# Softmax sum by identity matmuls, bf16 exponentials, other masks, two q,k loads and a new operation order in a one-core attention and mixer block

## The chip, the cores and the metric

The kernel runs on one core of a Trainium2 chip. The metric is the device time of one execution in microseconds (us); the median of a few executions is given. One further execution is recorded by the hardware profiler, and all rows of the profile come from that one. The core has five engines with a queue each: PE (matmuls; its weight loads appear as PEld), DVE (VectorE), ACT (ScalarE), POOL (GpSimd) and SP, which here issues the DMAs. Each engine works through its queue in order and waits on semaphores.

## The reference

Sequence length is 2048, width 448, all inputs and the output bf16. It is a pre-layernorm block with attention over a dilated window and then a mixer with an MLP:

```python
def _A_ref(x, wqkv, wo):                       # x is layernorm(A_x)
    H = 16; Dh = D // H                        # Dh = 28
    W, dil = 8, 2
    q, k, v = qkv[0], qkv[1], qkv[2]           # from x @ wqkv
    idx = pos[:, None] - (jnp.arange(W) * dil)[None, :]
    mask = idx >= 0
    logits = jnp.einsum("bhsd,bhswd->bhsw", q, kg) * scale      # kg = k at idx
    logits = jnp.where(mask[None, None, :, :], logits, -1e9)
    attn = _softmax(logits, axis=-1)           # over the 8 window entries
    o = jnp.einsum("bhsw,bhswd->bhsd", attn, vg)
    return o.reshape(B, S, D) @ wo
...
def _B_ref(x, w1, w2, w3, w4):                 # x is layernorm(h)
    h = _gelu(_layernorm(x) @ w1)
    hs = concat(four column groups of h, moved by 1, -1, 2, -2 rows) @ w2
    x1 = x + hs
    return x1 + _gelu(_layernorm(x1) @ w3) @ w4
...
h = x + _A_ref(_layernorm(x), A_wqkv, A_wo)
return h + _B_ref(_layernorm(h), B_w1, B_w2, B_w3, B_w4)
```

Only tokens 0 to 13 have window entries before the start of the sequence; for them the first-token mask matters.

## The kernel before

The 2048 rows are four tiles of 512. For each tile t these phases run: N1 (layernorm of x), A1 (q and k, transposed), V, A2 (logits), S (softmax), A3 (attention times v), O (wo and residual), B1 (second norm, w1 and gelu, called M). Then five units of 2, 4, 4, 4 and 2 row tiles of 128 go through B2 (the four shifted column groups times w2, and a norm called T), W3 (w3 and gelu into `h3T`) and B3 (w4 and the store).

**Recording and order.** Every phase first records operations (`S.add`, `S.group`); an operation is one instruction, or a group of matmuls. The list `ORDER` at the top of the file then gives one global sequence of operation numbers. `arrange` walks it, hands out buffers (8 PSUM banks, 3 `qk_r` buffers, 1 softmax buffer) and appends each operation to the queue of its engine, so `ORDER` decides what stands before what on PE, DVE, ACT, POOL and SP. `OTHER` lists operations that go to their alternative engine (an ACT copy to DVE, a DVE operation to POOL). All instructions are emitted at one line, L1014 (L1013 in the changed kernel), so the profile is read by names of tiles and by shapes.

**Pairs of half-height matmuls.** `duo` (L463) forms two outputs A and B whose contraction rows are split into upper and lower 64 partitions. Matmuls of the two halves alternate, so that they run as pairs, and a duo has two parts: in the second part the outputs change halves, and it waits by semaphore (`sdeps`) for the end of the first part. For V a duo is 8 matmuls and then 6; for q, k it is 8 and 6 per 512 columns. `ORDER` may put something else between the two parts, or nothing: then a row such as "x28" in the order of PE is two duos back to back.

**Softmax of a tile (L744 to L793).** A2 multiplies q by the eight shifted k on DVE (`qk_r`, 128x4096, in four chunks of channels, the last 128x2048), and PE sums over channels with the 0/1 matrix `zc` into one PSUM bank L (matmuls 128 rows by 32 columns of the array). For tile 0 the bank is started by a one-row matmul of `onesrow` and `maskrow` with 512 columns, which adds -30000 at the entries before the sequence. S takes the maximum on DVE (`mx<-ps`), subtracts (`ls<-ps,mx`), takes exp on ACT (`ls<-ls`, f32), sums over the window on DVE (`mx<-ls`), forms 1/sum as exp(-ln(sum)) on ACT (`mx<-mx`, twice), and multiplies on DVE (`pb<-ls,mx`). PE transposes `pb` with `ident` (80 columns), and the result is copied to `pt`.

**Attention times v.** A3 multiplies `pt` by a 0/1 band mask `bmask` on DVE (`bd_r`, 80x2048, four per tile) and PE multiplies `vw` by it in 32 matmuls (80 rows by 32 columns of the array). `bmask` is made at the start in `setup` (L609): POOL fills a table `par` (memset and one affine_select of 80x80), and two DVE reduces turn it into `bmask`.

**Loads.** SP issues, in this order, x in three DMAs (rows 0 to 511), q,k weights in four DMAs of 128x2x448 (two halves of the rows, q and k apart), x for tile 1 in two, v weights in two, and so on (from L436). In B2, units from the third on read shifted halves `ht`, which SP copies from `gT` (named `arena` in the trace) by seven DMAs.

## Time and profile before

| | value |
|---|---|
| median of 3 executions | 189.06 us (188.81 to 189.17) |
| the profiled execution's own time | 188.75 us |
| its span on the core | 187.0 us |
| PE busy | 179.8 us (96%) |
| DVE busy | 127.2 us (68%) |
| ACT busy | 121.8 us (65%) |
| POOL busy | 24.0 us (13%) |

The profiled execution took 188.75 us, of which 187.0 us are the span in which the core's instructions run and 1.75 us lie around it; it is 0.31 us below the median. PE is the busiest engine by far. DVE and ACT are full in the first 77 us, in which attention runs, and half empty after it. A row of the timeline gives the start, the length, the engine, the line, the operation with out<-in, the array tile (rows*columns) and the moving operand, a count, and in brackets the idle time before it with its releaser. Matmul records overlap: a duration in a row of one matmul includes the time in the array, so the pace of a run of matmuls is read from the starts of neighbouring rows.

### The profile page before, as it was taken

To read this page: it belongs to the slowest core of one execution; us is meant where nothing else is said; L and a number is where in the kernel's file an instruction comes from. 1 tells how busy PE (TensorE), PEld (TensorE's weight loads), DVE (VectorE), ACT (ScalarE), POOL (GpSimd) and SP (SyncE) were. 2 spreads that over 40 slices of the span, in tenths; PEclk is the share of its full clock that TensorE was granted. 3 is DMA by queue.
4 is the path that set the end of the run, shared out by engine and by line. 5 is a ranking of instruction groups with operands and counts; after the bars stand their busy time and mean duration, and the time that the engine had idled before them with its cause. 6 is when DMAs were issued, how large, how long until landed. Compare 5 with 4: busy or idle time off the path is not lost.

```text
span 187.0 us, 5780 instructions
## 1 busy us (share of the span) xinstructions
PE 179.8 (96%) x2496; PEld 93.4 (50%) x2496; DVE 127.2 (68%) x225; ACT 121.8 (65%) x289; POOL 24.0 (13%) x59
## 2 busy tenths in 40 slices
...
GB/s 153 314 297 189 14 91 124 186 192 34 154 75 112 112 227 160 298 52 101 16 112 7 38 25 22 94 133 53 35 40 40 116 0 46 112 0 4 49 98 49
DMA packets 34177, 18.59 MB, mean 99 GB/s; under 512 B 21240, under 2 KB 33640, under 8 KB 34152
## 3 DMA queue, kind: packets, MB, share of 16 engines
...
q8 instruction: 19, 0.31, 0.7%
q14 instruction: 6, 0.05, 0.1%
...
## 4 chain that ended last, share of the span: by engine, by line
PE 76%; DVE 14%; DMA 3%; SPq 3%; ACT 2%; issue 1%
PE ps L1014 76%; DVE qk_r L1014 9%; SPq L1014 3%; DMA xin<-in_A_x_dram 2%; DVE st L1014 2%; DVE lntm L1014 1%; ACT arena L1014 1%; DMA ht<-arena 1%; DVE mx L1014 1%; DVE ls L1014 0%; DVE pb L1014 0%; DVE mv L1014 0%; ACT actT L1014 0%; ACT rs_x L1014 0%; ACT rs_y L1014 0%
## 5 line engine op out<-in xcount | busy, mean ns | idle before, releaser
L1014 PE MATMUL ps<-actT,arena 64*128 64x512 bf16 (+2 forms) x812 | 69.6, 326 | 0.9 <-DMA arena<-in_A_wqkv_dram 0.5
L1014 ACT ACTIVATE h3T<-ps 128x512 bf16<-128x512 f32 (+1 forms) x70 | 30.9, 517 | 37.3 <-PE ps L1014 37.2
L1014 PEld LDWEIGHTS ps<-actT,arena 64*128 64x128 bf16 (+1 forms) x812 | 36.0, 96 | 30.9 <-PE ps L1014 1.9
L1014 PE MATMUL ps<-arena,h3T 64*128 64x448 bf16 (+3 forms) x434 | 44.7, 343 | 0.1
L1014 ACT ACTIVATE arena<-ps 128x512 bf16<-128x512 f32 (+6 forms) x66 | 30.6, 508 | 8.7 <-PE ps L1014 8.1
L1014 PEld LDWEIGHTS ps<-arena,h3T 64*128 64x128 bf16 (+1 forms) x434 | 22.3, 94 | 19.9 <-PE ps L1014 0.5
L1014 DVE TENSOR_TENSOR qk_r<-arena 128x4096 bf16<-128x4096 bf16 (+1 forms) x16 | 32.0, 2015 | 0.0
L1014 DVE SCALAR_TENSOR_TENSOR qk_r<-ps,mrs,arena 128x448 bf16<-128x448 f32 (+2 forms) x17 | 10.4, 653 | 30.8 <-PE ps L1014 30.8
L1014 POOL TENSOR_TENSOR arena<-arena,xin 128x448 f32<-128x448 f32 x16 | 16.1, 1033 | 78.6 <-ACT lntm L1014 66.0
L1014 DVE TENSOR_TENSOR bd_r<-arena,bmask 80x2048 bf16<-80x2048 bf16 x16 | 19.0, 1216 | 2.6 <-PE ps L1014 2.6
L1014 DVE SCALAR_TENSOR_TENSOR arena<-xin,rs_y,ps 128x448 f32<-128x448 bf16 x16 | 10.3, 673 | 11.6 <-PE ps L1014 11.5
L1014 PE MATMUL ps<-wo_s,actT 64*128 64x448 bf16 x128 | 14.5, 350 | 0.1
L1014 PE MATMUL ps<-actT,w_s 64*112 64x512 bf16 x112 | 13.8, 380 | 0.1
L1014 PE MATMUL ps<-w_s,arena 64*128 64x448 bf16 x83 | 12.8, 350 | 0.4 <-DMA ht<-arena 0.3
L1014 ACT ACTIVATE actT<-ps 128x512 bf16<-128x512 f32 (+2 forms) x20 | 12.3, 640 | 1.0 <-PE ps L1014 0.9
L1014 PE MATMUL ps<-arena,actT 64*128 64x448 bf16 x112 | 12.3, 351 | 0.2
L1014 ACT ACTIVATE lntm<-xin,nm 128x448 bf16<-128x448 bf16 x16 | 10.6, 666 | 1.4 <-DVE nm L1014 1.4
L1014 DVE BATCH_NORM_STATS2 st<-xin 128x6 f32<-128x448 bf16 x16 | 9.2, 613 | 1.3 <-DMA xin<-in_A_x_dram 1.3
L1014 ACT ACTIVATE rs_x<-mv,epsilon 128x4 f32<-128x4 f32 (+2 forms) x16 | 4.6, 297 | 7.4 <-DVE mv L1014 7.3
L1014 PEld LDWEIGHTS ps<-actT,w_s 64*112 64x112 bf16 x112 | 6.8, 127 | 5.2 <-ACT arena L1014 0.7
L1014 ACT ACTIVATE vt<-ps 128x448 bf16<-128x448 f32 x16 | 8.2, 544 | 1.2 <-PE ps L1014 1.1
L1014 PEld LDWEIGHTS ps<-w_s,arena 64*128 64x128 bf16 x83 | 5.5, 95 | 6.8 <-DMA ht<-arena 0.8
...
## 6 DMA issues: line engine op xcount, KB each, us to landing
...
```

Of the source, the lines that this page charges most:

```text
L1014: inst = getattr(eng, meth)(**kw)
```

## The change

The sum over the eight window entries leaves DVE: exp is written as bf16 (`es_b`), and eight matmuls with the full 128x128 `ident` as weights, 64 columns each, add the eight entries in PSUM. They write the first 64 columns of bank L, the bank that held the logits. ACT's logarithm reads the sum there, 1/sum is written as bf16 (`zr_b`), and the product `pb` reads two bf16 operands.

`bmask` is written by POOL alone: a memset and eight affine_selects of 80x64; the two DVE reduces are gone. The first-token mask becomes a matmul of 128 rows, 32 columns of the array and 98 moving columns inside the first logit group of tile 0 (`onesrow` and `maskrow` get 128 partitions, and only the first has ones and -30000). The q and k weights are loaded by two DMAs of 128x2x896.

`ORDER` is written anew for all engines; operation numbers differ by the recorded operations that were added and dropped. `OTHER` has three entries more (four are added and one is dropped): a second copy `actT<-ps` of tile 0's transposed norm and two small copies of 128x48 (`arena<-arena`) go from ACT to DVE, the multiplication `pb` of the last tile goes from DVE to POOL, and one copy of the last tile's `pt` stays on ACT.

```diff
--- before.py
+++ after.py
@@ -18,40 +18,40 @@
 RESIDUAL = 'ttvv'
 DENSE = 2
 ORDER = """
-2 5 6 0 1 41 42 43 8 9 7 10 52 53 54 57 12 13 14 4 55 56 58 15 16 35 44 31 64 62 38 39 17 45 65 63 36 46 59 60
...
+0 5 6 8 1 9 44 45 2 7 55 56 57 60 46 47 48 10 65 38 41 67 29 61 49 58 66 62 63 68 69 70 50 51 52 53 54 59 92 64
...
 """
 OTHER = """
-94 184 187 485 494 497 548 554
+97 99 186 189 238 350 484 493 496 550 556
 """
 FULL = (4,)
 FILL = (0, 0, 0, 0)
@@ -343,6 +343,8 @@
         epsilon = sb("epsilon", [128, 2], F32)
         mx = sb("mx", [128, NSM, 64], F32)
         ls = sb("ls", [128, NSM, 512], F32)
+        es_b = sb("es_b", [128, NSM, 512], BF16)
+        zr_b = sb("zr_b", [128, NSM, 64], BF16)
         zs = mx
         indj = ls[:, NSM - 1, 0:40].bitcast(BF16).rearrange("p (c h) -> p c h", c=5)
         pb = sb("pb", [128, NSM, NW * KW], BF16)
@@ -369,8 +371,8 @@
         kk = [arv(A_KV + t * KVB, 128, 3 * KVW).rearrange("p (c n) -> p c n", c=3) for t in range(NST)]
         kr = [arv(A_KV + t * KVB + 3 * KVW, 128, 4 * KW).rearrange("p (j n) -> p j n", j=4) for t in range(NST)]
         pt = [arv(A_KV + t * KVB + 4 * KVW, KW, 1024) for t in range(NST)]
-        maskrow = arv(A_KV + (NST - 1) * KVB, 1, 512)
-        onesrow = arv(A_KV + (NST - 1) * KVB + 512, 1, 32)
+        maskrow = arv(A_KV + (NST - 1) * KVB, 128, 512)
+        onesrow = arv(A_KV + (NST - 1) * KVB + 512, 128, 32)
         xb = [arv(A_KV + i // 4 * KVB, 128, 4 * D * 2).bitcast(F32).rearrange("p (i d) -> p i d", d=D)[:, i % 4, :] for i in range(NTL)]
 
         def shifted(t, c):
@@ -438,10 +440,7 @@
             load_x(i, 1)
         load_x(2, 2)
         act(zs[:, 0, 0:1], epsilon[:, 0:1], ACT.Exp)
-        for h in range(2):
-            for g in range(2):
-                dma("w%s%s" % ("qk"[g], "ab"[h]), wqkv_s[:, 2 * h:2 * h + 2, g * D:(g + 1) * D],
-                    A_wqkv[192 * h:192 * h + 256, g * D:(g + 1) * D].rearrange("(c k) n -> k c n", k=128), 256 * D * 2)
+        load_rows("wqk", wqkv_s[:, :, 0:2 * D], A_wqkv, 0, 2 * D)
         load_x(4, 2)
         load_x(6, 2)
         load_rows("wv", wqkv_s[:, :, 2 * D:3 * D], A_wqkv, 2 * D, D)
@@ -608,12 +607,10 @@
 
         def setup():
 
-            par = ls[0:KW, 0, 128:168].bitcast(BF16).rearrange("p (e j) -> p e j", e=2)
-            pool("memset", ap=par, constant=0.0)
-            pool("affine_select", out=par, in_=par, pattern=[[1, 2], [2, KW // 2]], compare_op=ALU.not_equal, fill=1.0, base=0, channel_multiplier=-1)
-            for e in range(2):
-                dve("tensor_reduce", out=bmask[:].rearrange("p (m e r) -> p m e r", m=4, e=2)[:, :, e, :],
-                    in_=bass.AP(par.tensor, par.offset + e * (KW // 2) + 1, [list(par.ap[0]), [8, 4], [1, NW], [1, 8]]), axis=AX.X, op=ALU.max)
+            pool("memset", ap=bmask[:], constant=0.0)
+            for w in range(NW):
+                pool("affine_select", out=bmask[:], in_=bmask[:], pattern=[[16, 4], [1, 2], [DIL, NW]], compare_op=ALU.not_equal, fill=1.0,
+                     base=DIL * (w + 1), channel_multiplier=-1)
             pool("memset", ap=indj, constant=1.0)
             for out_ap, pat, base in ((indj[:, 0:4, :], [[128, 4], [-DH, 16]], 0), (indj[:, 4, :], [[-DH, 16]], 320)):
                 pool("affine_select", out=out_ap, in_=out_ap, pattern=pat, compare_op=ALU.is_ge, fill=0.0, base=base, channel_multiplier=1)
@@ -635,7 +632,7 @@
             late("memset", ap=maskrow, constant=0.0)
             for w in range(1, NW):
                 lo = DIL * (NW - 1 - w)
-                late("memset", ap=maskrow[:, 0:64 * w].rearrange("p (r n) -> p r n", n=64)[:, :, lo:lo + DIL], constant=-30000.0)
+                late("memset", ap=maskrow[0:1, 0:64 * w].rearrange("p (r n) -> p r n", n=64)[:, :, lo:lo + DIL], constant=-30000.0)
             late("memset", ap=kk[0][:, :, 0:PADK], constant=0.0)
             late("memset", ap=kr[0][0:64, 0, 0:PADK], constant=0.0)
             late("memset", ap=vw[0:PADK, 0, 0, :], constant=0.0)
@@ -747,8 +744,6 @@
             sl = t % NSM
             held = []
             L = _Tile(P_bank)
-            if t == 0:
-                mm(L(lambda v: v[0:32, :]), onesrow[0:1, :], maskrow[0:1, :], True, False, 512)
             for c in range(4):
                 wide = 8 if c < 3 else 4
                 r = _Tile(P_qk)
@@ -762,7 +757,10 @@
                                       zc[:, c, e, :],
                                       r(lambda v, lo=lo: bass.AP(v.tensor, v.offset + lo + 64 * (NW - 1),
                                                                  [list(v.ap[0]), [16, 4], [-64, NW], [DIL, NW], [1, DIL]])),
-                                      c == 0 and e == 0 and not (t == 0 and j == 0), c == 3, 512, j))
+                                      c == 0 and e == 0, c == 3, 512, j))
+                if t == 0 and c == 0:
+                    first = lambda v: v.rearrange("p (r n) -> p r n", n=64)[:, 0:NW - 1, 0:DIL * (NW - 1)]
+                    terms.append((L(lambda v: first(v[0:32, :])), onesrow, first(maskrow), False, False, 98, 0))
                 op = mms(terms)
                 if t == NST - 1:
                     product_read.append(op)
@@ -773,13 +771,14 @@
             all_x = lambda v: y_e(v).unsqueeze(2).broadcast_to([128, 32, NW, DIL])
             dve("tensor_reduce", out=y_e(mx[:, sl, :]), in_=L(e_x), axis=AX.X, op=ALU.max)
             dve("tensor_tensor", out=x_e(ls[:, sl, :]), in0=L(x_e), in1=all_x(mx[:, sl, :]), op=ALU.subtract)
-            act(ls[:, sl, :], ls[:, sl, :], ACT.Exp, scale=SCALE)
-            dve("tensor_reduce", out=y_e(zs[:, sl, :]), in_=e_x(ls[:, sl, :]), axis=AX.X, op=ALU.add)
-            act(zs[:, sl, :], zs[:, sl, :], ACT.Ln)
-            act(zs[:, sl, :], zs[:, sl, :], ACT.Exp, scale=-1.0)
+            act(es_b[:, sl, :], ls[:, sl, :], ACT.Exp, scale=SCALE)
+            mms([(L(lambda v: v[:, 0:64]), ident[:], es_b[:, sl, :].rearrange("p (y x e) -> p x y e", x=NW, e=DIL)[:, x], x == 0, x == NW - 1, 64, None)
+                 for x in range(NW)])
+            act(zs[:, sl, :], L(lambda v: v[:, 0:64]), ACT.Ln)
+            act(zr_b[:, sl, :], zs[:, sl, :], ACT.Exp, scale=-1.0)
             row = lambda v, off, step: bass.AP(v, off, [[v.shape[1] * v.shape[2], 128], [step, NW], [16, 4], [DIL, NW], [1, DIL]])
-            mult = dict(out=row(pb, sl * NW * KW + DIL, KW + DIL), in0=row(ls, sl * 512, 64),
-                        in1=bass.AP(zs, sl * 64, [[64 * NSM, 128], [8, NW], [2, 4], [0, NW], [1, DIL]]), op=ALU.mult)
+            mult = dict(out=row(pb, sl * NW * KW + DIL, KW + DIL), in0=row(es_b, sl * 512, 64),
+                        in1=bass.AP(zr_b, sl * 64, [[64 * NSM, 128], [8, NW], [2, 4], [0, NW], [1, DIL]]), op=ALU.mult)
             S.add("dve", "tensor_tensor", alts=[("pool", [("tensor_tensor", mult)])], **mult)
             banks = [_Tile(P_bank), _Tile(P_bank)]
 
```

What the new order does is seen in the queues. In the rows, a shape is what the instruction writes, and x28 is a count of equal rows.

On PE at the start, from the first q,k matmuls of tile 0 (`ps<-actT,arena`) over V (`ps<-arena,actT`) to the first logit sums (`ps<-qk_r,zc`); before:

```order
L1014 MATMUL ps<-actT,arena 128x256 x72
L1014 MATMUL ps<-actT,arena 64x256 x28
L1014 MATMUL ps<-actT,arena 128x256 x6
L1014 MATMUL ps<-ident,lntm 128x64 x16
L1014 MATMUL ps<-actT,arena 128x256 x6
L1014 MATMUL ps<-ident,lntm 128x64 x16
L1014 MATMUL ps<-arena,actT 128x448 x28
L1014 MATMUL ps<-actT,arena 128x512 x28
L1014 MATMUL ps<-arena 32x512
L1014 MATMUL ps<-qk_r,zc 32x32x8x2 x8
```

and in the changed kernel:

```order
L1013 MATMUL ps<-actT,arena 128x256 x64
L1013 MATMUL ps<-arena,actT 128x448 x8
L1013 MATMUL ps<-actT,arena 128x256 x8
L1013 MATMUL ps<-arena,actT 128x448 x6
L1013 MATMUL ps<-ident,lntm 128x64 x32
L1013 MATMUL ps<-actT,arena 128x256 x12
L1013 MATMUL ps<-arena,actT 128x448 x14
L1013 MATMUL ps<-actT,arena 64x256 x16
L1013 MATMUL ps<-actT,arena 128x512 x8
L1013 MATMUL ps<-actT,arena 64x256 x40
L1013 MATMUL ps<-actT,arena 128x512 x8
L1013 MATMUL ps<-qk_r,zc 32x32x8x2 x8
```

V of tile 0, 28 matmuls in one piece before, now stands in pieces of 8, 6 and 14 among the q,k matmuls, and the q,k duos of tile 1 are split too. The mask matmul, ahead of the logit sums before, follows the last row shown.

On DVE, around the softmax of tile 0 and the products of tile 1; before:

```order
L1014 TENSOR_REDUCE mx<-ps 128x64
L1014 TENSOR_SCALAR nm<-mv 128x4
L1014 TENSOR_TENSOR ls<-ps,mx 128x512
L1014 TENSOR_TENSOR qk_r<-arena 128x4096
L1014 TENSOR_REDUCE mx<-ls 128x64
L1014 TENSOR_TENSOR qk_r<-arena 128x4096
L1014 TENSOR_TENSOR qk_r<-arena 128x2048
L1014 TENSOR_TENSOR pb<-ls,mx 128x8x64
L1014 TENSOR_TENSOR qk_r<-arena 128x4096
L1014 TENSOR_TENSOR bd_r<-arena,bmask 80x2048
```

and in the changed kernel:

```order
L1013 TENSOR_REDUCE mx<-ps 128x64
L1013 TENSOR_TENSOR qk_r<-arena 128x4096
L1013 TENSOR_SCALAR nm<-mv 128x4
L1013 TENSOR_TENSOR ls<-ps,mx 128x512
L1013 TENSOR_TENSOR qk_r<-arena 128x4096
L1013 TENSOR_TENSOR qk_r<-arena 128x2048
L1013 TENSOR_TENSOR pb<-es_b,zr_b 128x8x64
L1013 TENSOR_TENSOR qk_r<-arena 128x4096
L1013 TENSOR_TENSOR bd_r<-arena,bmask 80x2048
```

The reduce `mx<-ls` is gone, and the first product of tile 1 has moved ahead of the subtraction. On PE the eight sums of this tile (`ps<-es_b,ident`) stand between the first logit sums of tile 1 and the 28 q,k matmuls of tile 2.

On PE, where the third unit's shifted halves `ht` are first used; before:

```order
L1014 MATMUL ps<-actT,arena 128x512 x14
L1014 MATMUL ps<-bd_r,vw 32x64 x64
L1014 MATMUL ps<-wo_s,actT 128x448 x8
L1014 MATMUL ps<-actT,arena 128x512 x6
L1014 MATMUL ps<-wo_s,actT 128x448 x24
L1014 MATMUL ps<-w_s,arena 128x448
L1014 MATMUL ps<-w_l,ht 128x448
```

and in the changed kernel:

```order
L1013 MATMUL ps<-actT,arena 128x512 x8
L1013 MATMUL ps<-bd_r,vw 32x64 x64
L1013 MATMUL ps<-wo_s,actT 128x448 x8
L1013 MATMUL ps<-actT,arena 128x512 x6
L1013 MATMUL ps<-wo_s,actT 128x448 x24
L1013 MATMUL ps<-arena,h3T 128x448 x14
L1013 MATMUL ps<-w_s,arena 128x448
L1013 MATMUL ps<-w_l,ht 128x448
```

Fourteen matmuls of B3 (`ps<-arena,h3T`) now stand between the last wo matmuls of tile 3 and the first use of `ht`.

60 rows, old and new, of the table ORDER are left out of this document.

## The prediction

> **What bounds the kernel now.** I read the busy time by stretch first. The columns are the stretch, its length, and the busy time (with instruction counts) of PE, PEld, DVE, ACT and POOL, then the granted clock, the DMA share and GB/s.
>
> ```profile
> 8.30:35.00 26.70, 25.98 (x367) 13.18 (x367) 25.78 (x39) 23.12 (x63) 1.68 (x17) 1.00 0.66 152
> 35.00:62.00 27.00, 26.75 (x548) 12.68 (x552) 26.97 (x40) 24.78 (x67) 0.00 (x0) 1.00 0.55 118
> 62.00:77.00 15.00, 14.85 (x272) 7.98 (x265) 14.86 (x18) 14.68 (x34) 0.99 (x1) 1.00 0.76 193
> 77.00:110.00 33.00, 32.51 (x514) 18.16 (x514) 24.23 (x51) 24.73 (x53) 6.42 (x10) 1.00 0.31 75
> 110.00:184.60 74.60, 74.50 (x780) 39.15 (x776) 28.77 (x63) 30.29 (x66) 12.13 (x14) 1.00 0.25 54
> ```
>
> From 8.3 us to 184.6 us PE is idle for only 0.72 + 0.25 + 0.15 + 0.49 + 0.10 = **1.71 us**. So the time is PE's own work plus these 1.71 us, plus 8.3 us ahead of that and the 2.4 us up to the span's end at 187.0. The granted clock is 1.00 in every stretch. DVE is as full as PE between 8.3 and 77 us, so it can hold PE up there, but nowhere else. Next, pieces of the chain that ended last (start, length, what), and a row of PE's waits (total, times, longest):
>
> ```profile
> 28.25 0.59 DVE mx L1014
> ...
> 32.78 2.21 DVE qk_r L1014
> 34.99 0.04 issue
> 35.04 2.84 PE ps L1014 x58
> PE ps L1014 <- DMA ht<-arena: 0.3, 1, 0.3
> ```
>
> These chain rows stand where DVE hands over: up to 34.99 us DVE carries the chain, then PE. DVE time saved before 35 us can therefore move the end, and DVE time saved after that hardly at all.
>
> **The change part by part.** I count PE's own work first, then its idle time.
>
> *The pace of PE.*
>
> ```profile
> 13.85 0.40 PE L1014 MATMUL ps<-ident,lntm 64*128 64x64 bf16 x16
> 14.08 0.49 PE L1014 MATMUL ps<-actT,arena 64*128 64x256 bf16 x6
> ...
> 14.64 3.29 PE L1014 MATMUL ps<-arena,actT 64*128 64x448 bf16 x28
> 17.77 3.19 PE L1014 MATMUL ps<-actT,arena 64*128 64x512 bf16 x28
> 20.89 0.38 PE L1014 MATMUL ps<-arena 1*32 1x512 bf16 x1
> 21.20 0.62 PE L1014 MATMUL ps<-qk_r,zc 128*32 128x512 bf16 x8
> ...
> 38.68 0.42 PE L1014 MATMUL ps<-bd_r,vw 80*32 80x64 bf16 x32
> 39.03 0.93 PE L1014 MATMUL ps<-arena,actT 64*128 64x448 bf16 x8
> 71.22 0.43 PE L1014 MATMUL ps<-bd_r,vw 80*32 80x64 bf16 x32
> 71.47 0.63 PE L1014 MATMUL ps<-qk_r,zc 128*32 128x512 bf16 x8
> 115.01 6.78 PE L1014 MATMUL ps<-arena,h3T 64*128 64x448 bf16 x70
> 121.64 1.89 PE L1014 MATMUL ps<-actT,w_s 64*112 64x512 bf16 x16
> ```
>
> A pair of 448 columns costs (121.64 - 115.01)/35 = 0.189 us. Fourteen pairs of V should then take 2.65 us, but tile 0's V takes 17.77 - 14.64 = 3.13 us: 0.48 us more for two duos whose second part follows its first directly, 0.24 us each. That is what a duo pays when nothing stands between its parts, since the second part waits for the end of the first. A change of array shape costs about 0.10 us: 32 band matmuls take 0.35 us among half-height ones (38.68 to 39.03) and 0.25 us next to the logit sums (71.22 to 71.47), which have the same 32 columns.
>
> *Adjacent duo parts.* In the order of PE 12 duos have their parts directly behind one another before, and 6 do in the changed kernel. Six fewer at 0.235 us: **-1.41 us**. Below I take the new pieces between the parts to be long enough (8 to 28 matmuls) to cover the wait.
>
> *Identity sums.* 4 x 8 = 32 matmuls of 128x128 weights and 64 columns are added. No such shape is in the trace. From below: pairs of half-height matmuls of 64 columns pace at (14.08 - 13.85)/8 = 29 ns. From above, this row of PEld, whose columns are busy us, mean ns of one, and idle time:
>
> ```profile
> L1014 PEld LDWEIGHTS ps<-ident,lntm 128*128 128x128 bf16 x16 | 0.9, 98 | 1.8 <-DVE lntm L1014 1.7
> ```
>
> Sixteen full-height loads keep PEld busy 0.9 us, 56 ns each, under matmuls of 128 columns; one alone lasts 98 ns. So 29 to 56 ns if loads overlap as there, up to 98 ns if not: +0.93, +1.8 or +3.1 us. I take 29 ns, **+0.93 us**, since 128 columns explain the 56 ns of that row as well as its loads do.
>
> [...]
>
> *Array shapes.* PE changes shape 47 times before and 52 times after, since the sums stand among half-height matmuls: 5 x 0.10 = **+0.5 us**.
>
> *Mask matmul.* 512 columns took 21.20 - 20.89 = 0.31 us, of which 0.21 is its columns; 98 columns at the same rate are 0.04: **-0.17 us**. The next logit sums no longer stand behind it.
>
> PE's own work: -1.41 + 0.93 + 0.5 - 0.17 = **-0.15 us**.
>
> *The start.* PE waited 0.48 us at 8.32 for the last q,k weights:
>
> ```profile
> 8.32 5.69 PE L1014 MATMUL ps<-actT,arena 64*128 64x256 bf16 x106 [0.48 <-DMA arena<-in_A_wqkv_dram]
> 2.20 2.00 SPq L1014 DMA_DIRECT2D arena<-in_A_wqkv_dram  x4
> 6.86 1.62 ACT L1014 ACTIVATE actT<-ps 128x512 bf16<-128x512 bf16 x3 [0.20 <-PE ps L1014]
> ```
>
> Two issues of about 0.5 us each leave SP, so everything behind is issued some 1.0 us earlier, but the same bytes move. If the weights come earlier, the copies of the transposed tile 0 are next: ACT's end at 8.48. One of its three copies, 0.54 us each, goes to DVE, which brings this down. From -0.5 to +0.4 (a larger DMA that lands later as a whole); I take **-0.2 us**.
>
> *DVE up to 35 us.* The reduce at 28.25 goes, 0.59 us. More of the chain, and of PE's timeline:
>
> ```profile
> 13.98 0.32 issue
> 35.04 0.83 PE L1014 MATMUL ps<-qk_r,zc 128*32 128x512 bf16 x12 [0.21 <-DVE qk_r L1014]
> ```
>
> The chain's pause of 0.32 us at 13.98 is filled as well, since the new order puts four BN_STATS ahead of the first product where two stood. DVE gains 0.59 + 0.32 = 0.9 us by 35 us. PE can use only what it waits for there: 0.21 us for a product at 35.04, and its idle 0.72 us between 8.3 and 35 us. I take **-0.5 us**, between nothing and -0.7. DVE's work saved after 35 us I cost at nothing: its rivals there are PE's queue and the 0.25 + 0.15 us that PE idles.
>
> *The ht wait.* PE waited 0.32 us for `ht` at 109.28. Fourteen matmuls of B3, 7 x 0.189 = 1.3 us, now stand in front: **-0.3 us**, next late is nothing that the trace shows. A store now stands between SP's ht issues; at 0.5 us like the issues below, the 1.3 us cover it.
>
> *New waits.* PE now waits for exp at four points, and everything in its queue waits behind.
>
> ```profile
> L1014 DVE TENSOR_REDUCE mx<-ps 128x64 f32<-128x512 f32 x4 | 2.7, 680 | 0.0
> L1014 DVE TENSOR_TENSOR ls<-ps,mx 128x512 f32<-128x512 f32 x4 | 2.7, 680 | 0.0
> L1014 DVE TENSOR_TENSOR qk_r<-arena 128x4096 bf16<-128x4096 bf16 x12 | 27.2, 2281 | 0.0
> L1014 ACT ACTIVATE ls<-ls 128x512 f32<-128x512 f32 x4 | 2.5, 631 | 0.0
> L1014 ACT ACTIVATE mx<-mx 128x64 f32<-128x64 f32 x8 | 2.1, 262 | 0.1
> L1014 DVE TENSOR_TENSOR pb<-ls,mx 128x512 bf16<-128x512 f32 x4 | 2.7, 684 | 0.0
> L1014 DVE TENSOR_TENSOR bd_r<-arena,bmask 80x2048 bf16<-80x2048 bf16 x16 | 19.0, 1216 | 2.6 <-PE ps L1014 2.6
> ```
>
> The path from the last logit sum to the identity sums is maximum, subtraction and exp, 0.68 + 0.68 + 0.63 us; in tile 0 a product of 2.28 us stands before the subtraction, 4.3 us in all. PE's work meanwhile is 6 q,k matmuls, V of tile 1 and 8 logit sums: 3 x 0.216 + 14 x 0.189 + 0.6 = 3.9 us. Late by 0.4 us there. Behind the sums come Ln, exp (0.26 each) and `pb` (0.68) under other matmuls; in tile 1 two band products of 1.22 us may stand ahead of `pb` on DVE. From 0 to 1.4 us (0.35 at each of the four); I take **+0.5 us**, tile 0's 0.4 and a tenth.
>
> *Costed at nothing.*
>
> ```profile
> L1014 DVE TENSOR_REDUCE bmask<-ls 80x32 bf16<-80x256 bf16 x2 | 0.8, 394 | 0.0
> 12.01 1.32 DVE L1014 TENSOR_SCALAR lntm<-xin,mv,rs_y 128x448 bf16<-128x448 bf16 x4 [0.30 <-ACT rs_y L1014]
> L1014 POOL TENSOR_SCALAR_AFFINE_SELECT ls<-ls 80x80 bf16<-80x80 bf16 x1 | 0.3, 252 | 0.0
> L1014 POOL TENSOR_TENSOR arena<-arena,xin 128x448 f32<-128x448 f32 x16 | 16.1, 1033 | 78.6 <-ACT lntm L1014 66.0 <-DVE lntm L1014 12.7
> ```
>
> The two bmask reduces lay in pauses of DVE, one of them in its wait for ACT ahead of 12.01. POOL's mask in their place, nine operations of about 0.25 us, is due only with the first band product near 35 us, and POOL is busy for 1.68 us between 8.3 and 35. `pb` of the last tile on POOL (1033 ns for 448 columns, so about 1.2 us for 512, against 0.68) lies under 36 matmuls of W3, 18 x 0.216 = 3.9 us. Were these covers gone, each would cost its length, 0.5 to 2 us.
>
> Idle time and start: -0.2 - 0.5 - 0.3 + 0.5 = **-0.5 us**. With PE's own -0.15, the sum is **-0.65 us**: 188.75 - 0.65 = 188.10 us for the profiled execution, whose time stands 0.31 us under the median of 189.06, so **188.4 us** for the median.
>
> **The rivals.**
>
> *All waits vanish.* New waits are nil and the start gives 0.5: -0.15 - 0.5 - 0.7 - 0.3 = -1.65, so 187.4 us. For it: DVE sheds four reduces, 2.7 us. Against: four new points at which PE waits in order.
>
> *No gain.* The four new waits take 0.35 each, 1.4 instead of 0.5: 189.3 us; or the split duos still pay half of 1.41: 189.1 us. For it: the 4.3 against 3.9 us of tile 0, and that DVE is full to 77 us, so PE feels a late product. Against: DVE has 0.6 us less in each tile.
>
> *Slower: the weights of the identity sums aren't hidden.* 64 columns are too short to cover the load of 128x128 weights, and PE runs at the load's pace there, at four places per the order of PE: at 56 ns, +0.86, 189.3 us; at 98 ns, +2.2, 190.6 us. It decides from (0.65 + 0.38)/32 + 29 = 61 ns each, when the result is slower by more than 0.2%. For it: full weights last 98 ns alone. Against: 56 ns in a run.
>
> *The change doesn't do what it says.* If the semaphore between split parts were as costly with work in between, -1.41 would be lost: 189.8 us. Against: the 8 V matmuls at 39.03 are a part that stands alone, and their 0.93 us are four paces of 0.189 and the 0.16 us by which a single matmul's 0.35 exceeds one.
>
> **How the numbers follow.** Forecast 0.42 (187.9 to 188.8), all waits vanish 0.15 (187.2 to 187.9), no gain 0.23 (188.8 to 189.5), slower by weights 0.15 (189.2 to 190.6), parts still wait 0.05. The range is 187.2 to 190.0: it leaves out the upper end of the weights' case and little below. 0.2% is 0.38 us, about what a measurement of this kernel can tell from no change. Faster than 188.68 holds 0.36 of the forecast's share and 0.15, 0.51; slower than 189.44 holds 0.13 of the weights, 0.05 and 0.05 of no gain, 0.23; the rest, 0.26, is the same.
>
> **What would show it.** Eight `es_b` matmuls starting over 0.23 us (right), 0.45 us or more (weights). V of tile 0 without its extra 0.48 us. PE's idle time between its first q,k matmul and its last near 1.4 us instead of 1.71, with waits for exp about 0.4 us in tile 0 and under 0.1 us elsewhere. No wait for `ht`. If DVE still ends tile 1's products near 35 us, or PE's idle time exceeds 1.7 us, my account of waits is wrong; if PE's busy time grows by a microsecond, that of the matmuls is.

## The result and the profile after

The changed kernel takes **191.97 us** (191.67 to 192.38, 4 executions) against 189.00 us (188.81 to 189.17, 4 executions). The ratio is 1.0159, with a 95% interval of 1.0137 to 1.0181: slower by 3.0 us, where 0.65 us faster was forecast. Ratios here and below leave out single executions that took some per cent longer than the others of the same kernel at a lower granted clock. The profiled execution took 191.67 us, with a span of 190.0 us against 187.0.

First the same view of the changed kernel as for the one before, the busy time by stretch. The first stretch begins with its first q,k matmul and the last one ends with its last matmul:

```profile
8.06:35.00 26.94, 26.66 (x391) 13.63 (x393) 26.26 (x40) 23.24 (x63) 5.09 (x33) 1.00 0.64 157
35.00:62.00 27.00, 26.37 (x547) 13.01 (x544) 26.11 (x39) 25.35 (x66) 0.00 (x0) 1.00 0.46 107
62.00:77.00 15.00, 14.84 (x278) 8.67 (x275) 13.91 (x20) 14.33 (x32) 1.27 (x3) 1.00 0.87 215
77.00:110.00 33.00, 31.29 (x508) 18.00 (x504) 21.46 (x43) 24.12 (x53) 7.44 (x8) 1.00 0.32 68
110.00:187.50 77.50, 76.36 (x792) 40.10 (x788) 31.68 (x67) 31.92 (x68) 12.33 (x14) 1.00 0.25 52
```

The 3.0 us of the span divide as follows:

- PE starts on q,k at 8.06 instead of 8.32: -0.26 us.
- PE's busy time behind that start is 26.66 + 26.37 + 14.84 + 31.29 + 76.36 = 175.52 us. The same sum before was 174.59, so this is +0.93.
- PE's idle time is 0.28 + 0.63 + 0.16 + 1.71 + 1.14 = 3.92 us where it was 1.71: +2.21.

The last 0.1 us lie behind the last matmul. The granted clock is 1.00 in both. So the loss is idle time first, and work that was priced too low second.

Where it idles, by PE's waits (total, times, longest) in the changed kernel:

```profile
PE ps L1013 <- DVE arena L1013: 1.6, 1, 1.6
PE ps L1013 <- issue: 0.7, 2, 0.5
PE ps L1013 <- DMA w_l<-in_B_w_dram: 0.7, 1, 0.7
PE ps L1013 <- DMA actT<-lntm: 0.3, 1, 0.3
```

And PE's timeline at the places of which the prediction speaks:

```profile
11.57 0.92 PE L1013 MATMUL ps<-arena,actT 64*128 64x448 bf16 x8
12.32 0.60 PE L1013 MATMUL ps<-actT,arena 64*128 64x256 bf16 x8
...
20.27 0.21 PE L1013 MATMUL ps<-arena 128*32 128x98 bf16 x1
20.40 1.47 PE L1013 MATMUL ps<-actT,arena 64*128 64x512 bf16 x12
...
28.11 0.61 PE L1013 MATMUL ps<-qk_r,zc 128*32 128x512 bf16 x8
28.69 0.64 PE L1013 MATMUL ps<-es_b,ident 128*128 128x64 bf16 x8
29.26 3.19 PE L1013 MATMUL ps<-actT,arena 64*128 64x512 bf16 x28
...
46.84 0.36 PE L1013 MATMUL ps<-xin,ident 64*128 64x448 bf16 x2 [0.54 <-issue]
...
78.98 4.10 PE L1013 MATMUL ps<-actT,arena 64*128 64x256 bf16 x71 [1.65 <-DVE arena L1013]
...
112.75 0.36 PE L1013 MATMUL ps<-w_s,arena 64*128 64x448 bf16 x1 [0.68 <-DMA w_l<-in_B_w_dram]
165.30 2.02 PE L1013 MATMUL ps<-actT,arena 64*128 64x256 bf16 x28 [0.33 <-DMA actT<-lntm]
```

The duo of tile 0's V that was split now runs at the pace of a pair: eight matmuls in 12.32 - 11.57 = 0.75 us, four times 0.189. The mask matmul takes 20.40 - 20.27 = 0.13 us instead of 0.31. But an identity sum takes 29.26 - 28.69 = 0.57 us, and there are four. And there are two pauses in the middle, of 0.54 us at 46.84 and of 1.65 us at 78.98. They are new: no row of before has a wait at these matmuls. The groups of the new operations in the changed kernel:

```profile
L1013 PE MATMUL ps<-es_b,ident 128*128 128x64 bf16 x32 | 2.6, 237 | 0.0
L1013 DVE TENSOR_TENSOR pb<-es_b,zr_b 128x512 bf16<-128x512 bf16 x3 | 1.3, 422 | 0.4 <-ACT zr_b L1013 0.4
L1013 POOL TENSOR_TENSOR pb<-es_b,zr_b 128x512 bf16<-128x512 bf16 x1 | 1.2, 1206 | 7.5 <-ACT zr_b L1013 7.5
```

The 0.0 of the first row says that PE was idle ahead of none of the identity sums. `pb` takes 422 ns on DVE where it took 684 with both operands in f32, and 1.2 us on POOL as estimated.

**The pause at 78.98 has the wrong name.** The row puts it down to DVE's copy out of a PSUM bank, since that was the last semaphore of this matmul. DVE's copies there (DVE's timeline of the changed kernel) are:

```profile
76.39 1.26 DVE L1013 SCALAR_TENSOR_TENSOR arena<-xin,rs_y,ps 128x448 f32<-128x448 bf16 x2
78.22 0.66 DVE L1013 SCALAR_TENSOR_TENSOR arena<-xin,rs_y,ps 128x448 f32<-128x448 bf16 x1
```

The profile takes the copy that ended at 78.89, but the first of these three, which ended at 77.06, was enough: in the repaired kernel of the third group the same weight load starts at 76.80, when only the first had ended (at 76.74). So the bank was empty nearly two us before PE went on, and something else came last. The queues of the DMA engines show what. First a row of the changed kernel's page (packets, MB, share of the 16 engines), then the same columns for the stretch 71.4 to 75.8 us, which has a first queue only, and for 75.8 to 77.6 us (a packet counts whole in the stretch in which it starts, so a share can pass 100%):

```profile
q8 instruction: 20, 0.33, 0.7%
```

```profile
q1 hardware_dynamic: 1241, 1.11, 95.7%
...
q1 hardware_dynamic: 361, 0.33, 107.3%
q8 instruction: 1, 0.02, 5.9%
```

By its count the second queue carries **PE's own instructions**: 20 packets of 16,384 bytes for the some 5,100 instructions of PE, so 256 instructions each. A matmul and its weight load are two, and 47 semaphore instructions in PE's queue count as well. In the list of the starts of all of them the largest pauses behind 8 us and before the end are these:

```
changed kernel: instructions issued so far, rest after division by 256, pause between two starts
2497  193   77.06 -> 78.97   1.91 us
3552  224  111.73 -> 112.75  1.02 us   (w_l)
1473  193   45.95 -> 46.83   0.88 us
4583  231  164.59 -> 165.29  0.71 us   (transposed actT)
```

Both unexplained pauses are at a multiple of 256 plus 193, which looks like the end of a block (the other two are waits of the list above, for operands). With the packets beside them a sequence shows: there are 20 block ends and 20 packets, each packet starts between 1.6 us ahead of its block end (six of them do) and 4.4 us behind it, and the two unexplained pauses come at the block ends after the two whose packets started latest (2.4 and 4.4 us behind). So I read a packet as due when PE crosses one end, and needed at the next. The page gives both queues as shares of the same 16 DMA engines. End 2241 was crossed at 71.41; its packet started at 75.83 only and was done at 77.52, while the engines were 95.7% busy with data up to 75.8 us. PE had run out at 77.06, and went on 1.45 us after the packet's end. The data ahead of it are the halves of w4 (784 KB each), which SP now issues here (SP's timeline of the changed kernel):

```profile
69.09 0.77 SPq L1013 DMA_DIRECT2D arena<-in_B_w_dram  x1
69.91 0.75 SPq L1013 DMA_DIRECT2D vw<-vt  x1
70.70 0.61 SPq L1013 DMA_DIRECT2D arena<-in_B_w_dram  x1
71.36 3.04 SPq L1013 DMA_DIRECT2D w_l<-in_B_w_dram  x2
```

Before, the same loads stood further apart and later, and the packet got through in time. SP's timeline of the kernel before:

```profile
71.58 0.91 SPq L1014 DMA_DIRECT2D arena<-in_B_w_dram  x1
72.54 1.65 SPq L1014 DMA_DIRECT2D vw<-vt  x1
74.23 1.55 SPq L1014 DMA_DIRECT2D arena<-in_B_w_dram  x1
```

and of its DMA queues in the stretch 74.4 to 75.5 us:

```profile
q8 instruction: 1, 0.02, 5.5%
```

The block end was crossed at 72.08, the packet ran from 74.44 to 75.40, and the next end came at 78.42 without a pause. The pause at 46.84 is alike: crossed at 42.20, packet from 44.64 to 45.56 behind a transposing DMA that SP issues at 40.58 now and at 43.34 before; PE ran out at 45.95.

The theory to test: **late instruction packets**, called the fetch theory below. The rivals: the PSUM bank that the profile names (bank theory), and for the work the weights of the identity sums, as in the prediction.

### The profile page after: what moved, and what is told of

Same layout as the page of the kernel before. It is cut to its first block, busy times and chain, and to the rows that moved or that the text cites. A ratio compares the mean times of both kernels' runs of the same rounds, so it can differ in the third digit from the quotient of the medians.

```text
span 190.0 us, 5846 instructions
## 1 busy us (share of the span) xinstructions
PE 181.8 (96%) x2528; PEld 96.0 (51%) x2528; DVE 125.7 (66%) x220; ACT 122.8 (65%) x287; POOL 27.8 (15%) x67
## 4 chain that ended last, share of the span: by engine, by line
PE 83%; DVE 5%; ACT 4%; DMA 3%; SPq 1%; issue 1%; POOL 1%; POOLq 0%; DVEq 0%
PE ps L1013 83%; ACT arena L1013 2%; DMA actT<-lntm 2%; SPq L1013 1%; DVE lntm L1013 1%; DVE arena L1013 1%; DMA w_l<-in_B_w_dram 1%; ACT actT L1013 1%; DVE st L1013 1%; DVE bd_r L1013 1%; DVE qk_r L1013 1%; POOL rs_y L1013 0%; ACT lntm L1013 0%; POOL ident L1013 0%; ACT h3T L1013 0%
## 5 line engine op out<-in xcount | busy, mean ns | idle before, releaser
L1013 ACT ACTIVATE h3T<-ps 128x512 bf16<-128x512 f32 (+1 forms) x70 | 31.8, 513 | 41.5 <-PE ps L1013 41.0
L1013 PE MATMUL ps<-arena,actT 64*128 64x448 bf16 x112 | 13.1, 350 | 0.2
L1013 PE MATMUL ps<-actT,w_s 64*112 64x512 bf16 x112 | 13.0, 378 | 0.0
L1013 ACT ACTIVATE actT<-ps 128x512 bf16<-128x512 f32 (+2 forms) x19 | 11.8, 643 | 0.6 <-PE ps L1013 0.6
L1013 DVE TENSOR_SCALAR lntm<-arena,mv,rs_y 128x512 bf16<-128x512 f32 x14 | 8.2, 643 | 2.6 <-POOL rs_y L1013 2.0
```

The source lines that it names most:

```text
L1013: inst = getattr(eng, meth)(**kw)
```

## The experiments

Ratios are to the kernel before on the same chip, with 95% intervals; runs of one group share it. "Stop" is the pause between two starts of PE at a block end, in the one profiled execution of a kernel. Numbers in the diffs are operations of the order: 538 and 539 are the halves of w4, 531 and 532 the last two pieces of w_l.

### First group: the changed kernel with one thing moved

**One half of w4 later.** Only the second half goes behind the w_l pieces (`w_l` holds the weights that are multiplied with `ht`; SP loads it in seven pieces).

```diff
-568 584 397 539 533 531 574
+568 584 397 533 531 539 574
```

> The changed kernel with one DMA moved: the second half of the w4 load (784 KB) goes behind the last two w_l pieces in SP's queue; every other queue is as in the changed kernel. Fetch theory: PE stood still from 77.07 to 78.97 us because the next 16 KB of its own instructions came late; that packet started only at 75.83, 4.4 us after it fell due, behind two w4 halves on the DMA engines. With one half ahead of it, as before the change, it should start by 74.5, the stop of 1.9 us should shrink to 0.3 or less, and the time falls by 1.5 to 1.9 us (ratio to the kernel before about 1.006 to 1.008). Rival, bank theory: PE waited for DVE to empty a PSUM bank (the releaser that the profile names, a DVE write of arena ending at 78.9). DVE's queue is untouched, so the stop stays at 1.6 to 1.9 us and the time within 0.3 us of the changed kernel's.

Measured 196.18 us (192.69 to 197.06); even the fastest of the four is no gain. The packet started 6.2 us after its block end (77.99), with the first half still issued ahead of it, and the stop grew to 3.2 us. A miss: moving one half isn't enough. Behind this stop the granted clock was 0.50 for 3.4 us (0.991 over the span); what that adds to the time no run shows.

**DVE's bank emptied earlier.** A norm statistics operation of DVE (0.63 us) that stands ahead of the last of the three copies goes behind it, which serves the bank theory.

```diff
-604 605 389 558 596 553
+604 389 558 596 605 553
```

> The changed kernel with two instructions of DVE's queue swapped: the statistics (0.63 us) that stood between the third and the fourth emptying of a PSUM bank near 78 us go behind the fourth, so that the bank comes free 0.55 us earlier. Bank theory: PE's stop near 77 us shrinks from 1.9 to about 1.3 us and the time by 0.55 us. Fetch theory: the stop stays within 0.2 us of 1.9 us and the time is the same.

Measured 192.83 us (192.08 to 193.34), ratio 1.0184 [1.0128, 1.0241]: no gain. PE still stopped at count 2497, from 77.2 to 78.73, with the packet from 75.83 to 77.09. The bank theory's half microsecond didn't come in the time. The stop itself was 1.51 us, 0.4 shorter and so between the two expectations; but the packet ended 0.43 us earlier too, and PE resumed 0.34 us behind the moved copy (78.39). This run alone doesn't decide.

**The late w_l piece early.**

```diff
-533 531 574
+533 531 532 574
...
-669 532 410
+669 410
```

> The changed kernel with one small DMA moved: the 16-row piece of w2 (w_l) that SP issued at 110.84 us, behind the seven ht copies, goes to the other w_l pieces near 74 us. The changed kernel's PE waited 0.84 us at 112.75 for that piece. If the piece alone was late, the wait falls to 0 to 0.3 us (the last ht copy landed at 111.55, PE was ready at 111.9) and the time by 0.5 to 0.8 us. If ht is late as well, the wait changes its releaser and stays above 0.4 us.

Measured 193.96 us (two executions at 191.5 and 191.9, two at 196), ratio 1.0128 [1.0049, 1.0207]. The wait for w_l went, and `ht` took its place. The page's row of the clock (tenths of full speed in 40 slices) and two rows of PE's waits, of the profiled execution at 196.0 us:

```profile
PEclk9999999999999999669999999999999999999999
```

```profile
PE ps L1012 <- DVE bd_r L1012: 3.2, 1, 3.2
PE ps L1012 <- DMA ht<-arena: 0.6, 1, 0.6
```

The stop was 3.4 us here, with one more small load ahead of the packet (77.83 to 79.28); whether that load made it longer isn't shown, as the run with one half of w4 moved had a stop of 3.2 us without it. The granted clock was lowered to 0.50 for 6.8 us from 79.2 us on, two slices of 0.6 in the row.

**Identity sums undone.** DVE sums `es_b` again, in the new order; PE has 32 matmuls less.

```diff
-            mms([(L(lambda v: v[:, 0:64]), ident[:], es_b[:, sl, :].rearrange("p (y x e) -> p x y e", x=NW, e=DIL)[:, x], x == 0, x == NW - 1, 64, None)
-                 for x in range(NW)])
-            act(zs[:, sl, :], L(lambda v: v[:, 0:64]), ACT.Ln)
+            dve("tensor_reduce", out=y_e(zs[:, sl, :]), in_=e_x(es_b[:, sl, :]), axis=AX.X, op=ALU.add)
+            act(zs[:, sl, :], zs[:, sl, :], ACT.Ln)
```

> The changed kernel with the softmax sum back on DVE: one reduce of es_b (128x512, bf16) in the place of the eight identity matmuls of each tile; exp and 1/sum stay bf16, and the order of everything else stays. Each group of eight took 0.57 us on PE and about 0.1 us for the changes of array shape, 2.7 us in all, where the prediction had 0.93 + 0.5. If these sums are a main part of the loss, PE's busy time falls by 2.3 to 2.7 us and the time by 1.5 to 2.7 us, less what four reduces of 0.68 us on a full DVE give back (up to 1 us). If DVE is the limit there, the time stays within 0.5 us. PE's instruction stream is 64 shorter, so a late instruction block would meet PE elsewhere; that part is open in this run.

Measured 194.56 us (194.06 to 195.04), ratio 1.028 [1.0214, 1.0345], slower than the changed kernel itself. PE's waits for ACT's copies came up (1.5 and 1.3 us). I read this as an order that needs the DVE time that the identity sums give back; no run tests that reading. The stop at count 2497 was there too (1.0 us, packet from 78.97 to 80.18), on other matmuls.

### Second group: both halves of w4, and the kernel before

**Both halves of w4 behind w_l.**

```diff
-606 538 572
+606 572
...
-397 539 533 531 574
+397 533 531 538 539 574
```

> The changed kernel with both halves of the w4 load moved behind the last w_l pieces in SP's queue; the earlier run moved only the second half, and the first (issued 1.4 us ahead of the moment at which PE's next instruction block fell due) still held that block up, by 6.2 us. Fetch theory: with neither half ahead of it, the block's packet starts by 74.5 us instead of 75.8 to 78.0, PE's stop near 77 us falls from 1.9 to 3.4 us to 0.4 us or less, the granted clock stays at 1.00, and the time falls to a ratio of 1.003 to 1.009 to the kernel before. Bank theory (DVE empties a bank late): stop and time stay as in the changed kernel, 1.013 to 1.018.

Measured 190.86 us (190.01 to 191.68), ratio 1.0102 [1.006, 1.0143], 1.1 us below the changed kernel, a little less than expected. The packet ran from 74.51 to 75.78 and the pause at 2497 was 0.09 us. The one at 1473 remained (1.0 us), and in the profiled execution PE's first q,k matmul came at 8.79 us, 0.7 later than in the changed kernel.

**The kernel before with its w4 halves early.** 536 and 537 are the halves there.

```diff
-475 532 556
+475 532 537 536 556
...
-389 390 537 567
+389 390 567
...
-550 574 536 583
+550 574 583
```

> The kernel before with its two w4 halves moved ahead of three vw copies in SP's queue, so that both are issued just before PE's instruction block falls due at 72.0 us, as in the changed kernel; nothing else differs. Fetch theory: the block's packet starts at 76 us or later instead of 74.4, lands after 77, PE comes to the end of its instructions at 78.1 us and stops there for 0.4 to 1.5 us, at an instruction count that is a multiple of 256 behind the earlier block ends; the time rises by 0.4 to 1.5 us, ratio 1.002 to 1.008. Bank theory: no engine's queue but SP's is touched, and the copies arrive long before they are used (PE reads vw of tile 3 near 98 us), so no stop and no change.

Measured 189.31 us (188.67 to 189.49, and one of 194.33 among ten), ratio 1.001 [0.9993, 1.0026]. A miss: the packet moved from 74.44 to 75.67, as it should, and ended at 76.62, but PE reached the next end at 78.75 only, so nothing was late. A packet that ended 1.2 us later, and 2.1 us ahead of that end, cost nothing here.

**Three moves at once.** Both halves of w4 behind w_l, the late w_l piece early, and the transposing DMA ahead of the pause at 46.84 held back behind a matmul.

```diff
-606 538 572
+606 572
...
-397 539 533 531 574
+397 533 531 532 538 539 574
...
+        S.ops[439].deps.add(S.ops[270])
```

> The run with both w4 halves last, and two more moves on SP: the late w_l piece goes to the others (as in the run that moved it alone), and the DMA transpose that was issued at 40.6 us waits for a band product that ends near 43.5 us, so that it no longer stands ahead of PE's instruction block that falls due at 42.2 us. Fetch theory: PE's stop of 0.54 to 0.9 us at 46 to 47 us, which has no semaphore, goes as well; the wait at 112.75 falls from 0.84 to 0.5 to 0.75 us with ht as its releaser. Together 0.6 to 1.0 us below the run with w4 last, ratio 0.998 to 1.005. If the stop at 46 us has another cause it stays, and the transpose, 3 us later, may make PE wait near 53 us.

Measured 193.99 us (192.38 to 194.4), ratio 1.0252 [1.0206, 1.0298]. The stop at 1473 went (packet from 44.03), as the theory says, but PE then waited for the transpose itself:

```profile
PE ps L1013 <- DMA actT<-lntm: 3.3, 2, 2.9
```

A bad trade of my own making: 0.9 us gained, 2.9 paid.

**Identity sums in the kernel before,** for tiles 0 to 2, in its own order.

```diff
...
+            if t < NST - 1:
+                mms([(L(lambda v: v[:, 0:64]), ident[:], es_b[:, sl, :].rearrange("p (y x e) -> p x y e", x=NW, e=DIL)[:, x], x == 0, x == NW - 1, 64, None)
+                     for x in range(NW)])
...
```

> The kernel before with the identity sums alone, for tiles 0 to 2 (with all four no PSUM bank is left for W3): exp is written as bf16, and eight identity matmuls stand where DVE's reduce stood; tile 3 keeps the reduce. Price theory: each group costs PE 0.57 us and 0.14 us behind it, 2.1 us for three, and DVE's relief of 3 x 0.68 us gives 0.6 us back before 35 us and little after: +1.0 to +1.8 us, ratio 1.005 to 1.010. Relief theory: DVE is full up to 77 us and holds PE all along, so 3 x 0.68 us come back there: within 0.4 us of the kernel before. As PE's instructions get 48 more, a block may fall due at another time; a stop without a semaphore would show that.

Measured 191.47 us (190.91 to 192.07), ratio 1.0135 [1.0109, 1.0161], so +2.5 us. More than expected. Three sums of 0.57 are 1.7 us; waits for exp (0.4 us) and for `actT` (0.6 and 0.5) come on top, and a pause of 0.42 us at count 2497 (79.71), 1.56 us behind a packet's end. The identity sums cost in either order.

### Third group: the test of the fetch theory, and a repair

**More instructions ahead of everything.** The 11 warm-up matmuls become 33 short ones: 44 instructions more on PE before it has anything to do. If stops belong to matmuls, they stay at their matmuls; if to block ends, they move to the matmuls that now stand at 193 plus a multiple of 256.

```diff
-            return mm(busy(), ident[:], bass.AP(ident, 0, [[128, 128], [0, 4], [1, 128]]), True, True, 512, after)
+            return mms([(busy(lambda v: v[:, 0:170]), ident[:], bass.AP(ident, 0, [[128, 128], [0, 2], [1, 85]]), True, True, 170, None)] * 3, after)
```

> The changed kernel with its 11 warm-up matmuls of 512 columns at the start of PE's queue cut into 33 of 170 columns, the same work within a percent but 22 matmuls with their weight loads, 44 instructions, more; every other instruction of every queue is the changed kernel's. Fetch theory: PE's instructions come in blocks of 256, so each block end now stands 44 instructions earlier in the program. PE's stop near 77 us, which came 8 matmuls into W3 of the first unit, comes before W3, inside the band matmuls near 76 us, again at a count that is a multiple of 256 behind the earlier ones, and lasts until about 79 us (2 to 3 us); the stop at 46.8 us moves or goes likewise. Time within 1 us of the changed kernel's, ratio 1.010 to 1.022. Bank theory: the stop stays at the second duo of W3, behind its first 8 matmuls, whatever the count.

Measured 193.69 us (192.83 to 195.64), ratio 1.0269 [1.0205, 1.0333]. PE's waits and timeline of this run:

```profile
PE ps L1013 <- issue: 3.4, 4, 1.1
...
42.98 0.72 PE L1013 MATMUL ps<-wo_s,actT 64*128 64x448 bf16 x5 [0.75 <-issue]
...
47.62 0.21 PE L1013 MATMUL ps<-bd_r,vw 80*32 80x64 bf16 x2 [1.07 <-issue]
...
78.00 0.35 PE L1013 MATMUL ps<-bd_r,vw 80*32 80x64 bf16 x21
78.81 0.27 PE L1013 MATMUL ps<-bd_r,vw 80*32 80x64 bf16 x11 [0.46 <-issue]
```

The pauses now cut groups of equal matmuls in two (30 + 2, 21 + 11), where no operand and no bank changes. They come behind 1217, 1473, 2497 and 2753 instructions, each 193 plus a multiple of 256, and PE resumes 1.2 to 1.4 us after its packet's end where that can be read (46.38 to 47.62, 84.15 to 85.38). The wait by the name of DVE is gone: here the profile shows "issue". The time is above the expected 1.010 to 1.022; the stop at 2497 shrank to 0.65 us, but those at 1217 and 2753 are new. **The fetch theory holds and the bank theory falls.**

**Three repairs.** In the changed kernel, both halves of w4 and the w_l piece in the order w_l, w4; and four of DVE's norm operations of the last unit ahead of B3's output sums, for the wait at 165.30.

```diff
-606 538 572
+606 572
...
-397 539 533 531 574
+397 533 531 532 538 539 574
...
-831 737 832 738
+831 737 832 833 834 835 836 738
...
-777 833 834 798
+777 798
...
-734 835 785 836 799
+734 785 799
...
-669 532 410
+669 410
```

> The changed kernel with three repairs of order and no other edit: both w4 halves and the late w_l piece behind the other pieces on SP, and on DVE the second emptying of the last unit's B2 with its statistics ahead of three output sums of B3, which waited for PE until 155 us and held the last transposes up (PE waited 0.5 to 0.9 us for them at 165.3). Expected of each: the stop near 77 us gone (-1.9), the wait at 112.75 down from 0.84 to 0.25 to 0.75 us for ht, the wait at 165.3 gone (-0.5). Together -2.5 to -3.2 us from 191.97: 188.8 to 189.5 us, ratio 0.999 to 1.003, with the stop at 46.8 us (0.5 to 0.9) still in it. If the ratio stays above 1.006, the price of the identity sums weighs more than the stops.

Measured **189.27 us** (188.75 to 190.0, 10 executions), ratio 1.002 [0.9998, 1.0042]. PE's waits:

```profile
PE ps L1012 <- issue: 0.4, 2, 0.3
PE ps L1012 <- DMA ht<-arena: 0.4, 1, 0.4
```

and PE's timeline where the changed kernel stopped for 1.9 us:

```profile
76.43 3.79 PE L1012 MATMUL ps<-actT,arena 64*128 64x256 bf16 x66 [0.16 <-issue]
```

The packet ran from 72.77 to 73.97 and the pause at 2497, inside this row, was 0.09 us. No instruction differs from the changed kernel, only the order; 1.0159 to 1.002 are 2.6 of the 3.0 us.

### Fourth group: the price of an identity sum, on top of the repairs

**Half-height sums.** Each matmul becomes two on 64x64 quarters of the array, with a quarter of the weights each.

```diff
-            mms([(L(lambda v: v[:, 0:64]), ident[:], es_b[:, sl, :].rearrange("p (y x e) -> p x y e", x=NW, e=DIL)[:, x], x == 0, x == NW - 1, 64, None)
-                 for x in range(NW)])
+            steps([(h, dict(out=L(lambda v, part=part: v[part, 0:64]), lhsT=ident[part, part],
+                            rhs=es_b[part, sl, :].rearrange("p (y x e) -> p x y e", x=NW, e=DIL)[:, x], start=x == 0, stop=x == NW - 1), 64)
+                   for x in range(NW) for h, part in enumerate((TOP, BOT))])
```

> The run with three repairs, and each identity sum cut into two 64x64 matmuls on the two diagonal quarters of the array (rows and columns 0 to 63, and 64 to 127), which can run side by side: 16 matmuls of 64 columns for a tile in the place of 8 with full weights, the same sums. If the full 128-column weights set the pace (60 ns each where 64 columns alone would be 27), a pair takes about 29 ns as the half-height transposes do, a group 0.25 us instead of 0.57, and the time falls by 1.0 to 1.3 us below the run with three repairs: 187.9 to 188.4 us, ratio 0.994 to 0.999. If the pace comes from anything else (the accumulation into one bank, the wait for exp), a group stays above 0.45 us and the time within 0.4 us of that run. The 32 instructions more ahead of 46 us move that stop by 0.4 us at most.

Measured 191.81 us (190.36 to 193.06), ratio 1.0133 [1.0093, 1.0172]. A group still took 0.58 us:

```profile
29.77 0.65 PE L1013 MATMUL ps<-es_b,ident 64*64 64x64 bf16 x16
30.35 2.98 PE L1013 MATMUL ps<-actT,arena 64*128 64x512 bf16 x26
```

So the width of the weights doesn't set the pace. The loss against the repairs is again fetching in the main: 64 more instructions, and stops of 1.7 us at 47.93 and 1.3 us at 84.67.

**Four loads of q,k** as before, instead of two.

```diff
-        load_rows("wqk", wqkv_s[:, :, 0:2 * D], A_wqkv, 0, 2 * D)
+        for h in range(2):
+            for g in range(2):
+                dma("w%s%s" % ("qk"[g], "ab"[h]), wqkv_s[:, 2 * h:2 * h + 2, g * D:(g + 1) * D],
+                    A_wqkv[192 * h:192 * h + 256, g * D:(g + 1) * D].rearrange("(c k) n -> k c n", k=128), 256 * D * 2)
```

> The run with three repairs, with the q and k weights loaded by four DMAs again instead of two; all queues but SP's first rows are the same. If the two larger DMAs were worth the 0.2 to 0.3 us that the start seemed to gain, the first q,k matmul starts at 8.3 instead of 8.0 us and the time is 0.2 to 0.3 us longer. If they were worth nothing, both stay within 0.1 us; since DMAs at the start land up to 0.7 us apart from run to run, a difference below 0.2 us would not be told from none.

Measured 190.06 us (188.81 to 191.57, 12 executions), ratio 1.0047 [1.0018, 1.0076] against 1.002 for the repairs alone. The two large loads are worth 0.5 us of time by the medians; the intervals overlap. The first q,k matmul came at 8.48 instead of 8.03, but that shows little: in the 14 profiled executions here with two loads it came between 8.03 and 8.79.

**Neighbouring columns, and separate targets.** A sum reads every eighth pair of `es_b`: 32 pairs of bf16, 32 bytes from pair to pair. The first kernel reads 64 neighbouring columns instead, so it adds entries that don't belong together. The second leaves the reads and writes each matmul to columns of its own, so the log is taken of a single entry.

```diff
-            mms([(L(lambda v: v[:, 0:64]), ident[:], es_b[:, sl, :].rearrange("p (y x e) -> p x y e", x=NW, e=DIL)[:, x], x == 0, x == NW - 1, 64, None)
+            mms([(L(lambda v: v[:, 0:64]), ident[:], es_b[:, sl, 64 * x:64 * x + 64], x == 0, x == NW - 1, 64, None)
```

```diff
-            mms([(L(lambda v: v[:, 0:64]), ident[:], es_b[:, sl, :].rearrange("p (y x e) -> p x y e", x=NW, e=DIL)[:, x], x == 0, x == NW - 1, 64, None)
+            mms([(L(lambda v, x=x: v[:, 64 * (NW - 1 - x):64 * (NW - x)]), ident[:], es_b[:, sl, :].rearrange("p (y x e) -> p x y e", x=NW, e=DIL)[:, x], True, True, 64, None)
```

> The run with three repairs, in which each identity matmul reads 64 neighbouring columns of es_b instead of 64 columns in pairs with a step of 16 elements; it adds up entries that do not belong together, so the softmax is not the reference's. Everything else is equal. The matmuls of a group followed each other at 60 ns with strided columns, with full weights and with quarter weights alike. If the strided read sets that pace, it falls to 27 to 35 ns here and a group from 0.57 to 0.35 us or less; if not, it stays at 55 to 62 ns.

> The run with three repairs, in which the eight identity matmuls of a group write eight different stretches of 64 columns of the bank and add nothing up; the logarithm reads one entry instead of the sum, so the softmax is not the reference's. If adding to the same 64 columns sets the pace of 60 ns, it falls to 27 to 35 ns here and a group to 0.35 us or less. If the pace stays at 55 to 62 ns in this run and in the one with neighbouring columns, neither the read nor the target sets it.

One execution each: 189.35 and 189.20 us beside 189.26 of the kernel before. Separate targets leave the pace at 60 ns from start to start, and a group at 0.57 us. With neighbouring columns it is 29 ns and 0.34 us (timeline of that kernel):

```profile
29.03 0.41 PE L1012 MATMUL ps<-es_b,ident 128*128 128x64 bf16 x8
29.37 3.19 PE L1012 MATMUL ps<-actT,arena 64*128 64x512 bf16 x28
```

**The read with a step sets the price, not the weights and not the target.** The time didn't show it there, as that execution had a stop of 1.2 us at 47.27.

**Neighbouring columns, rightly.** ACT writes `es_b` so that each sum finds its 64 columns side by side, and `pb` reads the new layout. This kernel computes all of the reference.

```diff
-            act(es_b[:, sl, :], ls[:, sl, :], ACT.Exp, scale=SCALE)
+            act(es_b[:, sl, :].rearrange("p (x y e) -> p y x e", x=NW, e=DIL), x_e(ls[:, sl, :]), ACT.Exp, scale=SCALE)
-            mms([(L(lambda v: v[:, 0:64]), ident[:], es_b[:, sl, :].rearrange("p (y x e) -> p x y e", x=NW, e=DIL)[:, x], x == 0, x == NW - 1, 64, None)
+            mms([(L(lambda v: v[:, 0:64]), ident[:], es_b[:, sl, 64 * x:64 * x + 64], x == 0, x == NW - 1, 64, None)
...
-            mult = dict(out=row(pb, sl * NW * KW + DIL, KW + DIL), in0=row(es_b, sl * 512, 64),
+            mult = dict(out=row(pb, sl * NW * KW + DIL, KW + DIL), in0=bass.AP(es_b, sl * 512, [[512 * NSM, 128], [8, NW], [2, 4], [64, NW], [1, DIL]]),
```

> The run with three repairs, with exp written by ACT in another layout of es_b, so that the 64 columns that one identity matmul reads lie side by side; the multiplication pb reads the new layout, and all that is computed is the changed kernel's. By the look at neighbouring columns the eight matmuls take 0.34 us instead of 0.57, four times 0.23, and the 0.14 us behind them shrink too: -0.9 to -1.2 us against the run with three repairs (189.3), 188.1 to 188.5 us, ratio 0.994 to 0.999. If ACT writes the layout more slowly than 0.63 us, or DVE reads it more slowly than 0.43 us, part of that is lost in tiles 0 to 2; if PE's gain only lets it run into the stop at 47 us (1.04 us in that look), a quarter to a half of it.

Measured **188.89 us** (188.18 to 190.35, 12 executions) against 189.21 (23 executions), ratio 0.9994 [0.9969, 1.0019]: level with the kernel before, short of the expected 0.994 to 0.999, the best version found, and no shown gain. A group takes 0.34 us. The step has moved into `pb`, which takes 595 ns on DVE instead of 422, and exp takes 663 ns on ACT instead of 628.

**Five warm-up matmuls** instead of 11, 12 instructions fewer, so that end 1473 falls on a later matmul.

```diff
-WARM = 11
+WARM = 5
```

> The run with neighbouring columns, with 5 instead of 11 warm-up matmuls at the start. Fetch theory: 12 instructions fewer put the block end near 47 us 12 instructions later in the program, where PE needs some 0.04 us for each, while the block falls due in the band matmuls, where 12 instructions are 0.07 us: the stop of 0.4 to 1.0 us shrinks by 0.3 to 0.5 us and the time by as much. Rival: the warm-ups hold the granted clock up, and without them it falls below 1.00 in the first 40 us, or PE starts the first transposes late; then the time rises.

Measured 189.81 us (188.59 to 191.15, 12 executions), ratio 1.0042 [1.0016, 1.0069]. A miss: the stop at 1473 did go (crossed at 48.14 without a pause), but the start lost more and the time rose, as the rival said. Neither of its two reasons was seen: the granted clock was 1.000 over the span, and the first transposes start at 6.24 us, with eleven warm-ups at 6.27. The 64 first q,k matmuls, with five warm-ups and, below, with eleven:

```profile
8.21 5.28 PE L1012 MATMUL ps<-actT,arena 64*128 64x256 bf16 x64
13.32 0.92 PE L1012 MATMUL ps<-arena,actT 64*128 64x448 bf16 x8
```

```profile
8.12 3.67 PE L1012 MATMUL ps<-actT,arena 64*128 64x256 bf16 x64
11.62 0.92 PE L1012 MATMUL ps<-arena,actT 64*128 64x448 bf16 x8
```

5.11 against 3.50 us for the same work. With five warm-ups the first 32 follow each other at 105 ns and the other 32, from 11.58 us on, at 55; with eleven all 64 do at 55, and the pace doubled before them, at 7.2 us, among the transposes. So PE worked at about half pace up to 11.58 us with five warm-ups, which have a wait of 2.3 us behind them, and up to 7.2 us with eleven; what ends the half pace no run shows.

## Why the prediction was wrong

**What held.** The saving on split duos did: the first duo of tile 0's V lost its extra, and six duos with adjacent parts are left, at 0.23 us each (at 15.44, which is the second duo of that V, 25.87, 27.43, 109.83, 113.75 and 116.18), so the -1.41 stands. The mask gave -0.18 for -0.17. The start gave -0.26 for -0.2, but that may be luck, since starts with two loads lie 0.76 us apart from run to run. `pb` on POOL took the 1.2 us and hid. Up to tile 0's `pb` the kernel was ahead as forecast: its transposes start at 32.29 instead of 32.93.

**PE's own work, -0.15 forecast, +0.93 measured.** The term that was mis-sized is that of the identity sums, "I take 29 ns, +0.93 us", with four fifths of the array shapes' 0.5 behind the same four groups. Together that is 1.3 us; the groups took 4 x 0.57 = 2.3 us, 60 ns for each matmul. The rest of the terms adds up: -1.41 + 2.3 + 0.1 - 0.17 = 0.8 against 0.93.

The rival "weights not hidden" had the price about right (56 ns) and the reason wrong. Quarter weights left the 60 ns; neighbouring columns under the full weights gave 29 ns, and a group then took 0.34 us, or 4 x 0.34 = 1.4 us, which is the forecast. What was missed stands in the diff: the moving operand of the sum is read in pairs with a step. The row from which I took the 29 ns reads neighbours.

**Idle time and start, -0.5 forecast, +1.95 measured (+2.21 - 0.26).** This is the step that failed. The sum had terms for exp, `ht`, DVE and the start, and none for the order of the loads on SP between 66 and 76 us, which the change moves too; "next late is nothing that the trace shows" was said of `ht` alone, and looked only at operands. Late came:

- PE's instructions, twice: 1.65 and 0.54 us of idle time. Shown by the shifted program, in which the stops moved with the count, and by the repair, which removed one of them by order alone.
- The w_l piece, 0.68 us at 112.75, in the place of `ht`'s 0.32.
- The transposed tile at 165.30, 0.33 us.

The four new waits for exp, +0.5 us, cost nothing measurable: the groups of `es_b` have no idle time ahead of them. So that term erred the other way, and the idle time that DVE was to save did shrink, from 0.72 to 0.28 us before 35 us. The profile's own figures would have told the slack: the packet in the kernel before ended at 75.40, and PE ran into the next block at 78.42. With some 1.3 us between a packet's end and its use (1.2 to 1.6 in these runs) that left 1.7 us, and two loads of 784 KB moved ahead of it by 2.5 and 3.5 us.

Of the 20 block ends of the changed kernel 18 were crossed with at most 0.21 us between two starts of PE. The other two cost 0.88 and 1.91 us; ahead of the second the DMA engines were 95.7% busy with data for 4.4 us.

**The rivals.** "All waits vanish" and "parts still wait" are refuted, the second by the split duo of tile 0's V. "No gain" asked for late exp or halved savings; neither was seen. No rival had transfers in it, and so the range ended at 190.0.

**What stays open.** Why a packet is sometimes late by 2 us and sometimes by 6 behind similar loads wasn't settled; a load issued before the block end delayed it in each case seen, but I have no rule for how much. One stop remains in the best version (0.59 us at 46.56), as moving the transpose behind it cost more. How much the merged loads give was seen only with overlapping intervals. Which part of the read path makes the step expensive wasn't tried apart.
